# A RetNet and mixture-of-experts kernel: token tile 1 begun before expert 3 of tile 0, with batch 1's attention in token pairs

## The chip, the core and the metric

The kernel runs on one core of a Trainium2 chip. The core has a matrix engine (TensorE, PE in the profile), a vector engine (VectorE, DVE), a scalar engine (ScalarE, ACT), a general engine (GpSimd, POOL), a sync engine that issues transfers (SyncE, SP), and 16 DMA engines shared by all transfer queues. The metric is the device time of one execution in microseconds. It was 516.28 us, the median of six runs that lie between 514.69 and 517.29.

## What is computed

Two layers follow each other. The first is a retention attention over 8 batches, 8 heads, 576 positions and 64 dimensions: scores are multiplied by a decay instead of going through a softmax. The second is a mixture of four experts over the 4608 rows that come out, in which every expert works on every row.

```python
scores = scale * np.matmul(q, k.transpose(0, 1, 3, 2))
Dmat = np.where(rel >= 0, gamma[:, None, None] ** rel[None, :, :], 0.0)
attn = np.matmul(scores * Dmat[None], v)                 # [8, 8, 576, 64]
x = attn.transpose(0, 2, 1, 3).reshape(4608, 512)
p = domain_probs / (domain_probs.sum(-1, keepdims=True) + 1e-09)
for e in range(4):
    h = np.maximum(x @ w1[e], 0.0)                        # 512 -> 1024
    out += p[:, e:e + 1] * (h @ w2[e])                    # 1024 -> 512
```

## The kernel before

**Tiles and stages.** The 4608 rows are nine tiles of 512. A stage (nt, e) is one tile with one expert: the up product (512 to 1024 with ReLU, into the hidden tile `hT`) and the down product of the stage before, woven into it. A stage exists in two forms. The classical one (`up_classical`, `downs`) uses 32 products of 512 columns for up and 32 for down. The fast one (`up_fast`, `Down`) works by a seven-product scheme on halves of the matrices: 56 products of 256 columns each, with sums of the weights (`weight_sums`, `down_sums`), of the tokens (`token_sums`) and of the hidden tile (`hidden_sum`) that DVE makes. In `up_fast` each stage has two groups, and a quarter of the hidden tile gets its ReLU on POOL (the MIN/MAX in L716).

**Attention.** Chunks of 128 positions: scores (`S`), a mask, values (`O`), and a running state of keys times values (`sbd`), by which a later chunk sees the earlier ones. Four chunks make 512 positions and the remaining 64 (`Trem`, `Srem`, `Orem`) are handled apart. Class `Att` does whole chunks. Class `AttP` does token pairs: a unit is 256 positions (a half `hf`) by four heads (`u`), loaded with two neighbouring positions in a row of 512 bytes. Before the change only batch 0 is in pairs.

**What sets the order.** The order is written out by hand, engine by engine; each engine works through its own list, and a wait holds all that stands behind it on that engine. The head is the attention of batch 0, with warm-up products on PE between its parts (`warm`). Then classical stages run as a list of generators (`head`), counted in groups: one block of 128 hidden columns of an up product, or one block of 128 rows of a down product. `plan` and `at(g, ...)` hang other work behind group g, such as the casts, transposes and visits of batch 1 and the weight sums. From stage (1, 1) on a loop runs the fast stages. Between the quarters of a stage it calls `fill`, `sums`, `between` and `window`, which take attention work of batches 2 to 7 from lists (`Chain`) and the sums still owed from `owed`.

```python
begin = {1: (1, 1), 2: (1, 2), 3: (1, 3), 0: (2, 0)}
for nt, e in [(nt, e) for nt in range(1, n_nt) for e in range(E)][1:]:
    fast = before >= begin[before[1]]
```

**Transfers.** Weights are loaded on POOL's queue (fp32 in memory, bf16 on chip). Everything for tile 0's first stages and then all other experts is issued in one go at about 20 us. The inputs q, k, v go through SP's queue into buffers. Batch 0's remainder is gated on the landing of w2[0] and batch 1 follows it in order. Outputs are kept on chip over the four experts for tile 0 and the last tile (`on_chip`). For the others each stage sends its part, first plainly through SP, then by an accumulating transfer on POOL's queue (`send`).

## Time and profile before

| what | value |
|---|---|
| median of six runs | 516.28 us |
| the profiled execution, its own time | 515.51 us |
| its span, first to last instruction | 513.7 us |
| granted TensorE clock | 0.999 |
| instructions on PE, DVE, ACT, POOL | 4934, 696, 693, 345 |
| moved by DMA | 76.27 MB, 148 GB/s over the span |

The span is what the profile shows; the time of the execution is 1.8 us more. Profile times count from the span's start. In the lines of the profile, "L691" is line 691 of the kernel and "out<-in" names the tiles written and read. The page's busy times are sums over the whole span. The stretches (busy time of each engine between two times) show in their columns: the stretch, its length, PE, the weight loads of PE, DVE, ACT and POOL with the number of instructions, the granted clock, the share of the DMA engines and GB/s.

### The profile page before, as it was taken

The page shows a single profiled execution, that of the slowest core. Times are in us where ns is not written, and L with a number is a line of the kernel's source. Part 1 is how long each engine was busy: PE and PEld are TensorE (multiplying, and loading weights), DVE is VectorE, ACT ScalarE, POOL GpSimd, SP SyncE. Part 2 cuts the span into 40 slices and gives each one's busy share as a digit, 9 for nine tenths or more (in the row PEclk, how much of TensorE's full clock was granted, in tenths as well). Part 3 has the DMA queues.
Part 4 walks back from the last instruction along what each step waited for, and adds up shares of the span by engine and source line. Part 5 has one row for each costly group of instructions (what it writes and reads, how often), then busy time and mean ns, then how long its engine had stood idle before and what let it go on. Part 6 is the DMA issues. An engine that isn't in the chain of part 4 may idle for free.

```text
span 513.7 us, 12806 instructions
## 1 busy us (share of the span) xinstructions
PE 502.7 (98%) x4934; PEld 405.1 (79%) x4934; DVE 374.6 (73%) x696; ACT 336.1 (65%) x693; POOL 250.6 (49%) x345
## 2 busy tenths in 40 slices
PE   7999999999999999999999999999999999999995
PEld 3644455688888888888888888888888888888885
DVE  6625579778777777768777877886778777667775
ACT  3452254677667766777767776777777767767663
POOL 6702285656644756466645664476457521321012
PEclk9999999999999999999999999999999999999999
DMA  9999997949697699869998989789986652555002
GB/s 238 194 207 200 205 211 178 165 141 193 111 175 194 117 170 162 187 141 184 132 224 139 170 136 224 156 146 153 171 197 122 94 84 84 83 85 82 1 2 82
DMA packets 160749, 76.27 MB, mean 148 GB/s; under 512 B 131724, under 2 KB 144524, under 8 KB 160688
## 3 DMA queue, kind: packets, MB, share of 16 engines
q1 hardware_dynamic: 141648, 44.79, 43.7%
q0 software_dynamic: 18752, 30.41, 37.9%
q8 instruction: 38, 0.62, 0.5%
q10 hardware_dynamic: 288, 0.26, 0.2%
q14 instruction: 23, 0.19, 0.1%
HBM read 45.16 MB, written 31.46 MB: 149 GB/s over the span
## 4 chain that ended last, share of the span: by engine, by line
PE 91%; DVE 5%; DMA 1%; issue 1%; SPq 0%; ACT 0%; DVEq 0%; ACTq 0%
PE upP L691 21%; PE downV L645 20%; PE downW L645 15%; PE upR L691 10%; PE ph L525 7%; PE po L564 6%; PE upQ L691 5%; PE s L328 2%; PE oc L379 1%; PE kvp L346 1%; PE oc L376 1%; DMA raw<-in_q_dram 1%; DVE sT L469 1%; DVE sT L333 0%; DVE upR L707 0%
## 5 line engine op out<-in xcount | busy, mean ns | idle before, releaser
L691 PEld LDWEIGHTS <-wt 128*128 128x128 bf16 x992 | 94.9, 98 | 14.9 <-issue 1.9
L645 PEld LDWEIGHTS <-hT 128*128 128x128 bf16 x960 | 93.7, 98 | 12.0
L716 POOL TENSOR_SCALAR hT<-hT 128x512 bf16<-128x512 bf16 x62 | 38.2, 615 | 109.2 <-DVE hT L715 109.0
L645 PE MATMUL downV<-wt,hT 128*128 128x256 bf16 x480 | 81.8, 272 | 0.0
L691 PEld LDWEIGHTS <-wsum 128*128 128x128 bf16 x744 | 72.6, 98 | 9.1 <-issue 0.2
L707 DVE TENSOR_TENSOR upR<-upP,m 128x512 f32<-128x512 f32 x62 | 43.3, 698 | 49.0 <-ACT downW L651 39.9
L645 PEld LDWEIGHTS <-hsum 128*128 128x128 bf16 x720 | 70.0, 98 | 8.8 <-DVE hsum L617 0.3
L691 PE MATMUL upP<-xT,wt 128*128 128x256 bf16 x496 | 74.4, 272 | 1.1 <-DVE upR L707 0.6
L723 ACT ACTIVATE hT<-upP 128x512 bf16<-128x512 f32 x62 | 37.0, 597 | 52.0 <-PE upP L691 36.8
L514 POOL DMA_DIRECT2D out_dram<-acc x42 | 51.3, 1221 | 30.6 <-ACT acc L672 23.8
L674 DVE TENSOR_SCALAR acc<-downV,probs 128x512 f32<-128x512 f32 x56 | 41.9, 748 | 30.1 <-PE downV L645 29.7
L718 ACT ACTIVATE hT<-upR 128x512 bf16<-128x512 f32 x62 | 37.0, 597 | 31.7 <-PE upR L691 31.7
L709 ACT ACTIVATE hT<-upQ 128x512 bf16<-128x512 f32 x62 | 37.0, 597 | 15.9 <-PE upQ L691 15.9
L715 DVE TENSOR_TENSOR hT<-upP,m 128x512 bf16<-128x512 f32 x62 | 42.7, 689 | 6.0 <-PE upP L691 4.7
L672 ACT ACTIVATE acc<-downW,probs 128x512 f32<-128x512 f32 x56 | 38.6, 690 | 9.1 <-PE downW L645 9.1
L340 POOL TENSOR_SCALAR_AFFINE_SELECT sT<-sT 128x512 bf16<-128x512 bf16 x24 | 15.5, 646 | 58.0 <-ACT sT L339 48.6
L541 ACT ACTIVATE hT<-ph 128x512 bf16<-128x512 f32 x40 | 23.5, 597 | 29.8 <-PE ph L525 29.8
L697 ACT ACTIVATE upQ<-upP 128x512 f32<-128x512 f32 x62 | 37.0, 597 | 2.5 <-PE upP L691 2.3
L691 PE MATMUL upP<-tsum,wt 128*128 128x256 bf16 x248 | 37.3, 273 | 0.0
L691 PE MATMUL upR<-tsum,wsum 128*128 128x256 bf16 x248 | 37.2, 273 | 0.1
L691 PE MATMUL upP<-tsum,wsum 128*128 128x256 bf16 x248 | 37.2, 273 | 0.0
L691 PE MATMUL upQ<-xT,wt 128*128 128x256 bf16 x248 | 37.2, 273 | 0.0
(149 smaller groups left out, 1030.7 us busy)
## 6 DMA issues: line engine op xcount, KB each, us to landing
out_dram<-acc POOLq DMA_DIRECT2D x42, 512.0 KB, 6.4
out_dram<-acc SPq DMA_DIRECT2D x14, 512.0 KB, 4.1
wt<-in_moe_w_dram POOLq DMA_DIRECT2D x6, 1024.0 KB, 25.2
raw_k<-in_k_dram SPq DMA_DIRECT2D x24, 256.0 KB, 4.6
raw_q<-in_q_dram SPq DMA_DIRECT2D x24, 256.0 KB, 3.5
raw_v<-in_v_dram SPq DMA_DIRECT2D x24, 256.0 KB, 4.2
raw<-in_k_dram SPq DMA_DIRECT2D x8, 256.0 KB, 5.0
raw<-in_q_dram SPq DMA_DIRECT2D x8, 256.0 KB, 5.6
```

What stands on the lines that cost most here:

```text
L514: i = nc.gpsimd.dma_start(out=out_rows[:, x, :], in_=acc[nt, j], accum_op=ADD)
L645: nc.tensor.matmul(o, lhsT=l[:, k, self.s * 128:(self.s + 1) * 128], rhs=r[:, k], start=(i == 1 and k == 0), stop=(k == NFC // 2 - 1), ski ...
L672: nc.scalar.activation(a, po, Copy, scale=pe)
L674: nc.vector.tensor_scalar_mul(a, po, pe)
L691: nc.tensor.matmul(ps[:, l], lhsT=wa(kc)[:, f:f + 128], rhs=xa(kc), start=(start and l == 0 and kc == 0), stop=(kc == 1), skip_group_check ...
L697: nc.scalar.activation(Q, P, Copy)
L707: nc.vector.tensor_tensor(R_, P, m5, op=ADD)
L709: nc.scalar.activation(hT[:, lo, t0], Q, Relu)
L715: nc.vector.tensor_tensor(h22, P, m5, op=ADD)
L716: nc.gpsimd.tensor_scalar(h22, h22, float("inf"), 0.0, op0=MIN, op1=MAX)
L718: nc.scalar.activation(hT[:, lo, t1], R_, Relu)
L723: nc.scalar.activation(hT[:, hi, t0], P, Relu)
```

## The change

- Tile 0 runs experts 0, 1 and 2 classically. Then come stages (1, 0), (1, 1) and (0, 3), all fast, then (1, 2), (1, 3) and so on. Only the down product of (0, 2) is still classical beside a fast stage, with its quarters spread 8, 2, 2, 4 in the first group.
- Batch 1 is worked in token pairs by a new class `AttQ`. Its units are visited in the order 0, 2, 1, 3 (both halves of the first four heads, then of the others), between groups 25 and 31, and the last values product stands inside stage (1, 0).
- Batch 0's remainder moves from groups 29, 31, 34 to 22, 23, 24.
- The loads of batch 1 are gated on the first half of w1[2]. w2[2] is issued by POOL between two casts of batch 1, and w1[3] and w2[3] after its last cast. The raw buffers are taken from places that are free at that time.
- Batch 1's remainder is cast on POOL at the first gap of stage (1, 0). Batch 2's visits start after 16 gaps, which is in stage (0, 3).
- Weight and token sums get new places: those for experts 0 and 1 and tile 0 behind groups 9 to 31, those for experts 2 and 3 in stages (1, 0), (1, 1) and (0, 3).
- Outputs of tile 0 stay on chip for experts 0 and 1 only and are then sent; experts 2 and 3 are added by accumulating transfers.
- Eight more warm-up products stand in the head.

```diff
+    raw_x = xpool.tile([128, 2, H * D], FP32, tag="xT", name="raw")
     def raw_units(b):
         state[b] = {}
         for x in range(4):
-            t = wpool.tile([128, 3, H * D], FP32, tag=f"w2s_{x}", name="raw")
+            if b and x == 0:
+                t = [raw_x[:, 0], raw_x[:, 1], raw.tile([128, H * D], FP32, tag="raw", name="raw")]
+            elif b and x == 1:
+                t = [hpool.tile([128, H * D], FP32, tag=f"hs{i}", name="raw", bufs=1) for i in (1, 2, 4)]
+            else:
+                t = wpool.tile([128, 3, H * D], FP32, tag=f"w2s_{x}", name="raw")
+                t = [t[:, i] for i in range(3)]
...
+    class AttQ(AttP):
+        rem_states = (0, 1, 2, 3)
+        def visit(self, new, old):
+            ko = [one_bank(t, [128, 2, C + D], FP32, "ko") for t in ("a2", "o0")]
+            quads = [(a, j, d, c) for a in range(2) for j in range(2) for d in range(2) for c in range(2)]
+            if new:
+                hf, u = new
+                for a, j, d, c in quads:
+                    r, h = slice(64 * c, 64 * c + 64), 2 * a + d
+                    nc.tensor.matmul(ko[c][64 * d:64 * d + 64, a, C:], lhsT=self.m["k", hf, u][r, j, h, :],
+                                     rhs=self.m["v", hf][r, j, 4 * u + h, :], start=(a == 0 and j == 0),
+                                     stop=(j == 1), skip_group_check=True)
+                s = [one_bank(t, [128, 2, 2, C], FP32, "s") for t in ("a0", "a1")]
...
+            if old:
+                self.values(*old, ko)
...
-    def on_chip(nt):
-        return nt in (0, n_nt - 1)
+    def adds(nt, e):
+        return e > 0 and (nt == n_nt - 1 or (nt, e) == (0, 1))
+    def sends(nt, e):
+        return nt < n_nt - 1 and (nt, e) != (0, 0)
...
-    warm(8)
+    warm(10)
...
         a0.kv(hf, u)
+        if x < 3:
+            warm(2)
...
-    for e in range(2, E):
-        load_w1(e)
-        load_w2(e)
+    w12 = load_w1(2, 1)
+    load_w1(2, 0)
     load_next(w20)
...
-    for c in range(2):
-        for n in "kqv":
-            load_piece(1, n, c)
+    ORDER1 = (0, 2, 1, 3)
+    for x in ORDER1:
+        load_unit(1, x, w12)
...
-                    ok = n <= nt + 2
+                    ok = n <= (nt if (0, 3) in hTs else 0) + 2
...
+    at(3, lambda: cast1(0, "kv"), lambda: load_w2(2), lambda: cast1(1, "kv"), lambda: cast1(2, "kv"))
+    at(22, lambda: cast1(0, "q"), a0.Trem)
+    at(23, a0.Srem, a0.Srem_mask)
+    at(24, a0.Orem, lambda: a0.x(NCH, nc.scalar), lambda: a1.T(*UNITS[0]))
+    for i in range(4):
+        if i < 3:
+            at(24 + 2 * i, lambda i=i: cast1(i + 1, "q"))
+        at(25 + 2 * i, lambda i=i: visit1(i, i - 1))
+        if i < 3:
+            at(25 + 2 * i, lambda i=i: a1.T(*UNITS[ORDER1[i + 1]]))
+    at(25, lambda: cast1(3, "kv"), lambda: load_w1(3, 0), lambda: load_w1(3, 1), lambda: load_w2(3))
+    at(29, lambda: load_ahead(6))
...
+    stages = [(1, 0), (1, 1), (0, 3)] + [(nt, e) for nt in range(1, n_nt) for e in range(E)][2:]
+    owed = [((1, 0), (1, 1), t0[2])]
+    owed += [((1, 0), (1, 2), f) for f in ws[2][1:]]
+    owed += [((1, 0), (0, 3), f) for f in weight_sums(3)]
+    owed += [((1, 1), (1, 2), f) for f in down_sums(3)]
+    owed += [((1, 1), (1, 3), f) for f in down_sums(2)]
...
+            if gaps == 1:
+                rem1_casts()
+            if gaps == 13:
+                rem1_keys()
+            if i == 3 and gaps > 4:
+                pool(nt, 4 if gaps < 16 else 3 - g)
             if i == 3 or chain.todo["PE"] and "any" in chain.todo["PE"][0][1]:
-                chain.emit("PE", nt)
+                if gaps > 16:
+                    chain.emit("PE", nt)
...
+                for n in range((8, 2, 2, 4)[i - 1] if g == 0 else 4):
+                    if (g, i, n) == (0, 1, 4):
+                        visit1(4, 3)
+                        t1.pop(0)()
+                        front.extend(t1)
```

## The prediction

> **What bounds the kernel now.** I read the page's busy times and clock first, then busy time by stretch of the span, the chain of work, the DMA queues by stretch, and last the waits of GpSimd (POOL).

> ```profile
> PE 502.7 (98%) x4934; PEld 405.1 (79%) x4934; DVE 374.6 (73%) x696; ACT 336.1 (65%) x693; POOL 250.6 (49%) x345
> PEclk9999999999999999999999999999999999999999
> ```

> TensorE (PE) is busy all the time at the full clock. Where it has gaps is shown by the stretches (PE's busy time is the second number):

> ```profile
> 0.00:20.00 20.00, 15.58 (x229) 9.23 (x230) 13.80 (x35) 7.56 (x19) 14.95 (x31) 1.00 1.01 221
> 20.00:47.45 27.45, 27.45 (x142) 13.50 (x140) 9.45 (x16) 12.08 (x20) 5.47 (x7) 1.00 1.21 202
> 47.45:62.00 14.55, 14.55 (x89) 6.81 (x87) 7.36 (x14) 4.78 (x8) 1.83 (x3) 1.00 1.19 209
> 62.00:89.40 27.40, 27.16 (x245) 14.57 (x244) 23.40 (x36) 13.84 (x27) 18.91 (x21) 1.00 0.92 196
> 89.40:140.00 50.60, 49.77 (x481) 39.55 (x480) 41.04 (x71) 34.68 (x69) 30.94 (x40) 1.00 0.85 152
> 140.00:500.00 360.00, 359.62 (x3683) 314.19 (x3682) 271.35 (x509) 258.28 (x539) 175.07 (x241) 1.00 0.78 136
> ```

> From 20 us on PE loses 0.24 us before stage (1, 1) begins at 89.4, 0.83 us up to 140 and 0.38 us from there to 500. So the kernel gets faster by less PE work or not at all, and any new wait of PE adds to the time in full. The chain gives the prices of a piece:

> ```profile
> 33.64 13.81 PE po L564 x64
> 47.45 5.18 PE ph L525 x24
> 52.63 0.34 PE ptr L319 x8
> 65.63 0.45 PE ptc L309 x8
> 66.94 0.33 PE s L328 x8
> 67.27 0.24 PE kvp L346 x8
> 205.25 0.44 PE upP L691 x4
> ```

> A 512-column product takes 0.216 us (13.81/64), a 256-column one 0.109 (0.44/4). The third thing to see is how the two DMA queues share the engines; q0 carries the weights (issued by POOL), q1 what SP issues. The queues' packets, MB and share, first from 24 to 30 us, then from 42 to 46 us:

> ```profile
> q0 software_dynamic: 1233, 1.23, 124.0%
> ```

> ```profile
> q0 software_dynamic: 608, 0.62, 91.4%
> q1 hardware_dynamic: 606, 0.15, 29.4%
> ```

> Alone, the weights move 205 packets of 1 KB per us, 1 MB in 5 us. Shared, the queues go packet for packet, 152 per us each, so SP's small packets crawl. The last view is POOL's waits:

> ```profile
> POOL hT L716 <- DVE hT L715: 109.0, 41, 5.7
> ...
> POOL krb L287 <- DMA raw_k<-in_k_dram: 18.2, 1, 18.2
> ```

> POOL stood 18.2 us at one cast whose load crawled under the weights. It was harmless there, because the queue behind it was not urgent. The change puts POOL in that place again.

> **The change, part by part.**

> 1. *Fewer classical products.* Two up stages, (0, 3) and (1, 0), and the two down stages that belong to them become seven-product ones. Out go 120 products of 512 columns (25.9 us), 8 of 384 (0.163 each by their row, 1.3) and 8 of 128 (0.056, 0.45): 27.65. In come 224 of 256 columns: 224 x 0.109 = 24.45. That is -3.2 us, all on PE's path. [...]

> 2. *Batch 1 in token pairs.* Its 32 transposes stay 32. Scores were 32 products in four pieces of 0.33 (1.3 us); now they are 64, and batch 0's same form took 0.35 for 16 (1.4). Key-value products: 32 in four pieces of 0.24 (1.0) become 64 of 64 columns, between 0.24 and 0.35 per 16 (1.0 to 1.4). Values: 32 at 0.37 per 8 against 64 at 0.35 per 16, the same. State products go from 12 to 24 at 0.056 (+0.7). Batch 1's remainder reads four states instead of one: 12 x 0.029 = +0.35. Sum +1.2, between +1.0 and +1.7.

> 3. *Warm-up products:* eight more at 0.216, 1.7 us of PE in the head. Two stand before the first transposes, where PE waited 1.1 us for the query cast; the other pairs stand where it waited 0.57, 0.20 and 0.20. The two small waits are overrun by 0.23 each, but the transposes there feed a DVE that is still masking scores. Without that cover they cost 0.46. I take +0.1, between 0 and 0.5. They could also gain: the six runs lie at 514.7 to 514.9 and at 516.3 to 517.3, and one reading is a head that some executions run at a lower clock. The profiled execution shows no such drop, so I count nothing and keep -1.5 for the range.

> 4. *Old idle time:* the 0.24 us before 89.4 and the 0.4 us of the mask pile-up at 93.4 go, since batch 1 is finished before. The bulk payments of weight sums on DVE at about 112 us are replaced by similar ones. I take -0.6, between 0 and -1.

> 5. *Loads of batch 1.* All twelve are now wanted by PE at about 50 to 60 us instead of 65 to 77. They wait for the first half of w1[2]; the whole landed at 42.2 (issued 20.10, 22.1 us to landing), so that half lands at about 39.6. q0 runs dry at about 42. Batch 0's remainder (1536 packets of 256 bytes) is through by about 42.5. From there a 256 KB load takes 0.9 us: in the head q1 moved such packets at 297 GB/s. POOL casts the remainder and the first unit and issues w2[2] at about 47.3; its packets begin 2 us later, when seven loads are through. The other five share with w2[2]: 1024 packets at 152 per us are 6.7 us, in which two loads pass, then three more at 0.9. Landings: third unit's values 56.9, last unit's keys, queries, values 57.8, 58.7, 59.6. PE, without waits, starts up(0, 2) at 47.45 + 0.34 + 0.12 for the remainder moved ahead of it, and needs the third unit's cast values at 57.1 (6 x 0.86 of up, 0.55 remainder, 3 x 0.45 transposes, two visits 2.3). With POOL's cast of 0.61 it gets them at 57.5; the last unit's transposes then wait for DVE's query cast (58.7 + 0.75) about 0.3. I take +0.7, between 0 and +4 (the loads moved behind all of w2[2]).

> 6. *Remainder of batch 1 on POOL.* Its casts stand in front of the MIN/MAX of the first hidden tile of stage (1, 0). Behind that stand the hidden sums on DVE, behind them the DVE addition that frees PE's bank. On q1 two output sends stand ahead of its loads; 512 KB took 1.35 us there (0.38 MB/us at 105 to 108 us), so they are through at 61.3. w1[3] is issued after the last values cast, its packets begin at about 62.3. So one microsecond is left alone at 820 packets per us; the rest (about 700) shares, 4.6 us. The last piece lands at about 68. It is needed by 72: stage (1, 0) begins at 62.6, its last bank is wanted 12.6 later, less 0.4 cast, 0.6 MIN/MAX, 2 x 0.42 hidden sums, a 0.69 weight sum and the 0.69 addition. I take +0.1. If all 1536 packets share, or crawl as batch 0's did (10.2 to 16.3 us from issue), it is up to +5.

> 7. *First visit inside stage (1, 0):* last values to ScalarE copies (three, 0.25 to 0.38) to a 0.42 token sum to PE, against 0.86 + 0.44 of cover: +0.1. Weight sums of expert 3 want w1[3] at about 71; it lands at about 70. Four more POOL output sends (1.2 each) lie in POOL's idle half. The stages after (1, 1) keep their pattern of visits.

> Sum: -3.2 + 1.2 + 0.1 - 0.6 + 0.7 + 0.1 + 0.1 = -1.6 us. The profiled execution took 515.51, so it would take 513.9; the median of the runs shown is 0.77 above it, and against 516.28 I predict 514.6.

> **Rivals.** (a) *POOL stuck at batch 1's remainder*, slower: it decides as soon as the last piece lands after 72 us. Issued at about 61 and crawling like batch 0's values it lands at 77.3; cast, MIN/MAX, sums and addition end at 80.5 instead of 75.2. That is 5.3 us on -1.6: 520.0. For it: the 18.2 us row, and 2 MB of weights on q0 at that very time. Against: one microsecond of free queue is enough. (b) *Unit loads later*: w2[2] overtakes three more loads, and the last unit is 2 us later. This gives 516.7. For it: POOL may issue w2[2] earlier than I have it. Against: its issue waits for a cast that comes late in the same chain. (c) *Everything hidden*: parts 5 to 7 at zero and all old idle time gone, -3.0: 513.3. For it: my margins in parts 5 and 6 are under 1 us.

> **How the numbers follow.** A measurement of this kernel tells about 0.3% (1.55 us) from no change. Forecast 0.40, own range 513.4 to 515.6 (0.31 of it under 514.73, faster; 0.09 within). (c) 0.12, faster. (b) 0.18 (0.13 within, 0.05 slower). (a) 0.30, slower. So faster 0.43, within 0.22, slower 0.35. The range goes from (c) less half of the 1.5 us of part 3, 512.6, to (a), 520.0.

> **What would show it.** 224 more matmuls of 256 columns at 0.109 and 120 fewer of 512: part 1. PE's waits for DVE's query casts and for GpSimd's values casts near 57 to 60 us, together under 1 us: part 5. GpSimd's wait at krb and vbd ending before 72 us, and no DVE hidden sum that waits for GpSimd in stage (1, 0): part 6; a wait of several microseconds there is rival (a). Stage (1, 1) should begin at about 76.5 us; each microsecond later is a microsecond lost. The prediction is wrong if PE's gaps between 47 and 90 us add up to over 2 us.

## The result, and the profile after

The changed kernel is slower. Its median is 518.21 us (22 runs between 515.87 and 521.01) against 515.73 us of the kernel before (46 runs between 514.59 and 519.27); the ratio is 1.0052, with a 95% interval of 1.0040 to 1.0064. The prediction had been 514.6. The profiled execution took 519.62 us (its span is 517.9), where the prediction's sum had 513.9; it is 1.4 us above the median.

From the page of the changed kernel: busy times, the clock over the span, and the shares of the chain.

```profile
PE 505.0 (98%) x5150; PEld 416.6 (80%) x5150; DVE 383.9 (74%) x722; ACT 348.5 (67%) x736; POOL 252.9 (49%) x351
PEclk9999899999999999999999999999999999999999
PE 88%; DVE 4%; DMA 3%; issue 2%; ACT 1%; SPq 1%; POOL 0%; DVEq 0%; ACTq 0%; POOLq 0%
```

A digit 8 now stands in the fifth slice of the clock (about 52 to 65 us), and transfers have 3% of the chain. The stretches of the changed kernel, with PE's busy time second and the granted clock before the DMA share:

```profile
20.50:47.45 26.95, 26.95 (x141) 13.01 (x139) 17.63 (x30) 12.10 (x20) 5.35 (x8) 1.00 1.22 219
47.45:62.00 14.55, 10.85 (x207) 6.30 (x204) 6.88 (x14) 9.54 (x30) 5.87 (x7) 0.94 1.12 250
62.00:75.00 13.00, 12.36 (x131) 7.47 (x132) 7.03 (x15) 7.18 (x18) 5.85 (x9) 0.80 1.12 183
75.00:90.00 15.00, 14.77 (x116) 11.08 (x114) 14.01 (x22) 9.87 (x20) 10.31 (x10) 1.00 0.96 183
```

From 20.5 to 47 us PE loses nothing. Then it loses 3.7 us in one stretch and works with a clock of 0.94 and 0.80 in two. PE's waits from 20 to 100 us (total, times, longest):

```profile
PE pt L517 <- DVE qm L433: 3.8, 1, 3.8
PE upP L772 <- DVE hT L796: 0.7, 1, 0.7
PE upP L772 <- DVE upR L788: 0.5, 2, 0.3
```

The long one is that of the last unit's transposes (`pt`) for the query cast. The delay is 4.0 us, not 3.8: a product's recorded end lies 0.16 us behind the moment at which the next can start (eight `ph` products of 0.216 are recorded as 1.89 us and not as 1.73). From here on the text gives waits with these 0.16 us, and the lines show them without. The chain of work around it (start, length, what):

```profile
48.72 12.66 DMA raw<-in_q_dram
...
61.47 0.70 DVE qm L433
62.18 0.05 issue
62.22 1.03 PE pt L517 x8
63.25 3.41 PE ph L609 x8
```

The last unit's queries take 12.66 us from issue to landing, where those of the third unit take 5.4. The clock record shows half speed from 60.25 us, still in the wait, for 6.83 us: behind the wait eight `ph` products take 3.41 us where they otherwise take 1.73 (0.216 each), eight transposes 1.03 where they otherwise take 0.45. The queues from 50 to 57 us (packets, MB, share):

```profile
q0 software_dynamic: 825, 0.84, 83.4%
q1 hardware_dynamic: 780, 0.39, 26.1%
```

In those 7 us w2[2] on q0 and batch 1's loads on q1 go nearly packet for packet, but at 118 and 111 a us, not at the 152 of the prediction. Without w2[2] beside them, q1 moved 574 of these 512-byte packets from 49 to 50 us.

Stage (1, 1) starts at 82.57 us, where the prediction had 76.5. From there to the span's end it is 435.3 us (517.9 - 82.57), where the prediction had 435.6 (513.9 less the 1.8 outside the span, less 76.5). So the whole loss of this execution lies ahead of 82.6 us.

### The profile page after: what moved, and what is told of

The parts are those of the page before. It is cut to its first block, busy times and chain, and to the rows that moved or that the text cites. A ratio compares the mean times of both kernels' runs of the same rounds, so it can differ in the third digit from the quotient of the medians.

```text
span 517.9 us, 13354 instructions
## 1 busy us (share of the span) xinstructions
PE 505.0 (98%) x5150; PEld 416.6 (80%) x5150; DVE 383.9 (74%) x722; ACT 348.5 (67%) x736; POOL 252.9 (49%) x351
## 4 chain that ended last, share of the span: by engine, by line
PE 88%; DVE 4%; DMA 3%; issue 2%; ACT 1%; SPq 1%; POOL 0%; DVEq 0%; ACTq 0%; POOLq 0%
PE upP L772 22%; PE downV L726 21%; PE downW L726 16%; PE upR L772 11%; PE upQ L772 5%; DMA raw<-in_q_dram 3%; PE ph L609 3%; PE po L645 3%; PE s L340 2%; PE oc L391 1%; PE kvp L358 1%; PE oc L388 1%; DVE sT L482 1%; DVE upR L788 1%; SPq L113 1%
## 5 line engine op out<-in xcount | busy, mean ns | idle before, releaser
L772 PEld LDWEIGHTS <-wt 128*128 128x128 bf16 x1056 | 101.0, 98 | 16.7 <-issue 2.9
L726 PEld LDWEIGHTS <-hT 128*128 128x128 bf16 x1024 | 100.0, 98 | 12.8
L797 POOL TENSOR_SCALAR hT<-hT 128x512 bf16<-128x512 bf16 x66 | 41.3, 625 | 115.7 <-DVE hT L796 115.4
L726 PE MATMUL downV<-wt,hT 128*128 128x256 bf16 x512 | 87.2, 272 | 0.0
L772 PEld LDWEIGHTS <-wsum 128*128 128x128 bf16 x792 | 77.3, 98 | 9.6
L788 DVE TENSOR_TENSOR upR<-upP,m 128x512 f32<-128x512 f32 x66 | 46.1, 698 | 50.1 <-ACT downW L732 41.3
L726 PEld LDWEIGHTS <-hsum 128*128 128x128 bf16 x768 | 74.7, 98 | 9.1
L772 PE MATMUL upP<-xT,wt 128*128 128x256 bf16 x528 | 79.2, 272 | 1.0 <-DVE xT L676 0.5
L804 ACT ACTIVATE hT<-upP 128x512 bf16<-128x512 f32 x66 | 39.4, 597 | 53.7 <-PE upP L772 38.8
L598 POOL DMA_DIRECT2D out_dram<-acc x46 | 56.2, 1221 | 33.8 <-ACT acc L753 27.0
L755 DVE TENSOR_SCALAR acc<-downV,probs 128x512 f32<-128x512 f32 x60 | 44.9, 748 | 31.5 <-PE downV L726 31.0
L352 POOL TENSOR_SCALAR_AFFINE_SELECT sT<-sT 128x512 bf16<-128x512 bf16 x24 | 15.5, 646 | 59.2 <-ACT sT L351 50.3
L772 PE MATMUL upP<-tsum,wt 128*128 128x256 bf16 x264 | 39.6, 273 | 0.7 <-DVE hT L796 0.7
L772 PE MATMUL upP<-tsum,wsum 128*128 128x256 bf16 x264 | 39.6, 273 | 0.0
L772 PE MATMUL upR<-tsum,wsum 128*128 128x256 bf16 x264 | 39.6, 273 | 0.0
L772 PE MATMUL upR<-xT,wsum 128*128 128x256 bf16 x264 | 39.6, 273 | 0.0
L772 PE MATMUL upQ<-xT,wt 128*128 128x256 bf16 x264 | 39.6, 273 | 0.0
```

The source lines that it names most:

```text
L598: i = nc.gpsimd.dma_start(out=out_rows[:, x, :], in_=acc[nt, j], accum_op=ADD)
L726: nc.tensor.matmul(o, lhsT=l[:, k, self.s * 128:(self.s + 1) * 128], rhs=r[:, k], start=(i == 1 and k == 0), stop=(k == NFC // 2 - 1), ski ...
L755: nc.vector.tensor_scalar_mul(a, po, pe)
L772: nc.tensor.matmul(ps[:, l], lhsT=wa(kc)[:, f:f + 128], rhs=xa(kc), start=(start and l == 0 and kc == 0), stop=(kc == 1), skip_group_check ...
L788: nc.vector.tensor_tensor(R_, P, m5, op=ADD)
L797: nc.gpsimd.tensor_scalar(h22, h22, float("inf"), 0.0, op0=MIN, op1=MAX)
```

## The experiments

Times are medians of runs beside the kernel before on the same chip, with the ratio to it and its 95% interval. The theory: two sets of loads, batch 1's units (3 MB) and w2[2] (1 MB), are wanted by about 62 us, the transfers cannot bring both, and what comes last is waited for; the wait also halves PE's clock (for 6.83 us in the changed kernel). The first rival: the place of w2[2] in POOL's queue alone is at fault. Others are that the new PE work costs more than it was priced, and that the wait, not the clock, carries all of the loss.

**w2[2] later, and w2[2] first.**

```diff
# e1_w2_late
-    at(3, lambda: cast1(0, "kv"), lambda: load_w2(2), lambda: cast1(1, "kv"), lambda: cast1(2, "kv"))
+    at(3, lambda: cast1(0, "kv"), lambda: cast1(1, "kv"), lambda: cast1(2, "kv"), lambda: load_w2(2))
# e4_w2_first: taken out of at(3, ...), and
     load_w1(2, 0)
+    load_w2(2)
     load_next(w20)
```

> The load of w2[2] is issued behind the casts of batch 1's third unit instead of in front of those of the second; nothing is left out. Theory (w2[2] pushes the last unit's loads behind it, TensorE waits for the last query cast and then runs at half clock): the last queries land at about 55 us instead of 61.4, the wait of TensorE at the fourth transposes falls from 3.8 us to under 1, the clock stays at full, w2[2] lands at about 62 and costs at most 1 us at the first classical down product of stage (1, 0). Median about 514 us, 4 us under the changed kernel. Rival (the loss is in the paired attention or on GpSimd and the wait only shows it): stage (1, 1) still begins at 82 us or later, median 517 to 519.

> The load of w2[2] is issued with the first burst, right behind w1[2]; nothing is left out. Theory (the transfers are the limit: bytes of batch 1 and of w2[2] together must pass before the last queries): the last queries still land at 58 to 61 us, and the units before come later too; median 517 to 520. Rival (the order on GpSimd is the cause: its issue between two casts): the wait falls under 1 us and the median to about 514.

PE's longest wait in e1 and in e4:

```profile
PE po L645 <- DMA wt<-in_moe_w_dram: 4.1, 1, 4.1
```

```profile
PE sr L400 <- DVE kbd L315: 5.1, 1, 5.1
```

e1: 518.09, 1.0058 (1.0040 to 1.0076). The last unit's queries land at 53.7 and its transposes do not wait, but w2[2] lands at 65.57 and the first down product waits for it. e4: 519.99, 1.0093 (1.0072 to 1.0115). w2[2] is early, and the first unit is late: its queries land at 51.2. Their cast stands in VectorE's list ahead of the copies of batch 0's remainder (`kbd`), and PE waits for these from 47.5 us. These two places only choose who waits, and for them the rival falls.

**Filling the wait.**

```diff
# e2_fill_wait (18) and e7_fill_8 (8), ahead of the last unit's transposes
+            if i == 2:
+                at(29, lambda: warm(18))
             at(25 + 2 * i, lambda i=i: a1.T(*UNITS[ORDER1[i + 1]]))
```

> 18 warm-up products (3.9 us at full clock) stand in front of the fourth unit's transposes, where TensorE waits 3.8 us in the changed kernel; nothing else moves. Theory (the half clock after the wait is a cost of its own): the clock stays at full from 47 to 75 us, the transposes still come at about 62.2, stage (1, 0) begins at about 65.2 instead of 67.6, median 516. Rival (the low clock costs nothing, or it comes from something else than the wait): median 518 or more, the clock low as before.

> Eight warm products (8 x 0.216 = 1.7 us of TensorE work on constants) stand in front of the last unit's transposes, in the place of the first part of the 4.0 us wait. [...] Rival (the half clock is shown in the records but costs nothing, or the filler's own time adds): 518 or more, as with eighteen products.

e2: 518.23, 1.0061 (1.0046 to 1.0076). The clock stays at 1.0, and from the transposes to stage (1, 0) it is 3.1 us (63.10 to 66.19) against 5.4 in the changed kernel (62.22 to 67.61): the half clock costs 2.3 us there. Nothing is won, since in this execution the queries had landed at 58.4 and the filler itself was the delay. The clock is not all of the loss: seven of the 22 runs of the changed kernel have a mean granted clock of 0.998 or more (one stretch of 3.41 us at half speed takes 0.003), and they lie between 515.87 and 520.75 us, still above the 515.73 of the kernel before. e7: 517.67, 1.0056 (1.0026 to 1.0085). Stage (1, 1) starts at 79.50, 3.1 us earlier than in the changed kernel, and yet the time is nearly the same: a wait of 2.3 us at 91 us, with the clock at half for 3.4 us behind it, takes it back. This was the first sign of a second limit.

**The warm-up products.**

```diff
# e3_old_warm
-    warm(10)
+    warm(8)
-        if x < 3:
-            warm(2)
```

> The eight added warm-up products of the head are taken out again, all else as changed. Theory (they are hidden in waits of the head): the first up products begin within 0.2 us of the changed kernel's, median 518 give or take 0.7. Rival 1 (they delay the head): 0.5 to 1.7 us faster. Rival 2 (without them the head falls to a lower clock in some executions): 1 us or more slower.

518.49, 1.0067 (1.0043 to 1.0090), like the changed kernel: the eight products are not the loss.

**The load of w2[2] left out.** e5 fills the tile with a constant on VectorE at the start, e9 on GpSimd while it is idle.

```diff
# e9_no_w2_pool
     load_w1(2, 0)
+    w2_none = wpool.tile([128, NFC, Dm], BF16, tag="w2_2", name="wt2")
+    nc.gpsimd.memset(w2_none, 0.01)
     load_next(w20)
-    at(3, lambda: cast1(0, "kv"), lambda: load_w2(2), lambda: cast1(1, "kv"), lambda: cast1(2, "kv"))
+    at(3, lambda: cast1(0, "kv"), lambda: w2_sb.append(w2_none), lambda: cast1(1, "kv"), lambda: cast1(2, "kv"))
```

> Leaves out the load of expert 2's w2 (1 MB): its tile is filled with a constant by VectorE in the first microseconds, so expert 2's down products are computed with wrong weights but in the same number. Theory (two sets of loads, batch 1's units and w2[2], are both wanted by about 62 us, and the DMA engines cannot bring both): with 1 MB less in the queue the last unit lands by 55, neither the transposes of the last unit nor the first down products of expert 2 wait over 1 us, the clock stays 1.0, stage (1,0) starts at about 61 and stage (1,1) at 75.8 to 76.5. The profiled execution is 435.3 us from there to the span's end plus 1.7 outside it: 512.8 to 513.5, 1.5 to 2.5 us under the kernel before. Rival 1 (the token pairs of stage (1,0) or the visits themselves cost more than was priced): (1,1) starts at 78 or later and the time is over 515. Rival 2 (w2[2] has no part in the late landing; 512-byte pieces are slow by themselves): the queries of the last unit still land after 58, 517 or more.

> As e5_no_w2 (the load of expert 2's w2 left out, its tile filled with a constant, so the products of expert 2 are done with wrong weights), but the fill stands on GpSimd between 25 and 35 us, where it has nothing to do, and not ahead of VectorE's first work, where it put everything 3.9 us back. Theory: with 1 MB less, no wait over 1 us up to stage (1,1), which starts at 75.8 to 76.5; what then bounds is the chain of batch 2's loads, the value cast on GpSimd and the second output of (0,2) behind it near 92 us, which may take 0.5 to 2 us: 512.8 to 515. Rival (stages cost more than they were priced, whatever the loads do): (1,1) at 78 or later.

e5 misses: 516.69, 1.0014 (0.9995 to 1.0032). Its fill took 3.47 us ahead of VectorE's first work, and the first transposes began at 9.78 in place of 5.71. e9: 513.09, 0.9953 (0.9935 to 0.9970), faster than before. PE's waits from 40 to 100 us and two stretches of e9:

```profile
PE upP L772 <- DVE hT L796: 0.7, 1, 0.7
PE upP L772 <- DVE upR L788: 0.5, 2, 0.3
```

```profile
47.45:62.00 14.55, 14.46 (x278) 8.87 (x278) 10.24 (x20) 11.86 (x38) 11.54 (x13) 1.00 1.19 271
62.00:75.00 13.00, 12.57 (x104) 8.35 (x102) 9.72 (x19) 8.61 (x18) 2.41 (x3) 1.00 1.20 204
```

The wait and the half clock are gone and stage (1, 1) starts at 75.99. The 6.63 us between the two profiled executions (519.62 and 512.99) are 0.3 us in the head, 4.0 of wait and 2.3 of half clock. So the PE work is, in sum, what it was priced at, and 1 MB of transfers makes the difference.

**Keeping the outputs away from w2[2].**

```diff
# e6_w2_out1: as e1, and in send(); e8_w2_outs: without the j
             i = nc.sync.dma_start(out=out_rows[:, x, :], in_=acc[nt, j])
+            if (nt, e, j) == (0, 1, 1):
+                after(i, w2_dma[2])
```

> As e1_w2_late (w2[2] issued after the last unit's keys and values of the third visit are cast, 52.5 us), and the second output of (0,1), with batch 1's remainder behind it on SP's queue, starts only once w2[2] has landed. Theory: w2[2] then shares only with the last loads of the units and the first output, 1.5 MB from 53.5 at about 180 KB/us, and lands at 61 to 62 in place of 65.6, so the wait of 4.07 us at the first down product goes, the clock stays 1.0, (1,1) starts at 76 to 77, and the profiled execution is 513.3 to 514.5. Rival (the transfers are the limit wherever they stand): the second output lands at 66 or later and the accumulator that it frees, or the remainder of batch 1 after 72, takes over 2 us of the gain: 515.5 to 517.5.

> As e6_w2_out1, but both outputs of (0,1) start only once w2[2] has landed. Theory: w2[2] lands at 59 to 60, no wait at the down products; the first output lands at about 64.5 and its accumulator is wanted at about 62.5, so up to 2 us of wait comes there, without a drop of the clock: 514 to 516. Rival: the outputs and the remainder behind them come so late (the remainder over 72) that the time stays at 517 or more.

Both much worse: 524.21, 1.0159 (1.0142 to 1.0177), and 526.57, 1.0203 (1.0185 to 1.0222). The chain of e6:

```profile
64.64 13.09 DMA raw_q<-in_q_dram
77.73 0.07 issue
77.80 0.33 POOL qrb L301
```

w2[2] lands at 63.4 and is waited for by 0.7 us only. But the remainder of batch 1, behind the held output on SP's queue, now crawls beside the 2 MB of expert 3 and lands at 77.7. PE waits 6.3 us for what hangs behind it. In e8 the first output lands at 70.1, and PE already waits 5.4 us from 67 us on. The wait in e6 is the prediction's rival (a), produced by the gate.

**Fewer bytes: expert 2 of tile 0 added on chip.**

```diff
# e10_keep; e11_keep_late: the same with e1's line
-        return e > 0 and (nt == n_nt - 1 or (nt, e) == (0, 1))
+        return e > 0 and (nt == n_nt - 1 or (nt, e) in ((0, 1), (0, 2)))
-        return nt < n_nt - 1 and (nt, e) != (0, 0)
+        return nt < n_nt - 1 and (nt, e) not in ((0, 0), (0, 1))
-            i = nc.sync.dma_start(out=out_rows[:, x, :], in_=acc[nt, j])
+            i = (nc.gpsimd if (nt, e) == (0, 2) else nc.sync).dma_start(out=out_rows[:, x, :], in_=acc[nt, j])
```

> Expert 2 of tile 0 is added on chip to the accumulators of experts 0 and 1 (VectorE evacuates its products in place of ScalarE), so the two outputs of (0,1), 1 MB of writes between 50 and 65 us, go, and the outputs of (0,2) are plain writes. w2[2] stays where the changed kernel has it. Theory: the last unit's loads stand ahead of those outputs in one queue and gain little from it: the queries land at 60 to 61.4, the wait stays over 2.5 us, and the time is 516.5 to 518. Rival (the outputs share the engines with the last loads): the queries land by 59, the wait is under 1.5 us and the clock stays 1.0, 514 to 515.5.

> e10_keep and e1_w2_late together: no outputs of (0,1), and w2[2] issued at 52.5 us behind the casts of the third unit. In e1 its packets began to move only when the outputs' writes were through (55.9), and then shared with the remainder of batch 1 at 152 packets each a us. Theory: they begin at 54.6 and share with the remainder alone, 1024 packets at 152/us, so w2[2] lands at 61.5 to 62.7 and the first down product, wanted at 61.5, waits under 1.2 us; the clock stays 1.0, (1,1) starts at 76 to 77, and the time is 513 to 515. Rival (a wait moves further back: the remainder after 66, w1[3] after 71, or the accumulators near 92): over 516.

e10: 518.85, 1.0071 (1.0036 to 1.0106), above the range of either side. The queries land at 59.9 and the gap is 1.8 us, between the two expectations, and with VectorE's four evacuations come gaps of 1.2 and 1.1 us at 78 and 84 us. e11: 516.75, 1.0029 (1.0017 to 1.0041). The wait for w2[2], landed at 63.84, is 2.5 us with the clock at half for 3.4 us behind it, and the VectorE gaps are there too.

**w2[2] in two halves.** The first four down products need one half only.

```diff
# load_w2(e, part) loads blocks part * NFC // 2 to (part + 1) * NFC // 2; at(3, ...) becomes
# e12_split
+    at(3, lambda: cast1(0, "kv"), lambda: cast1(1, "kv"), lambda: load_w2(2, 0), lambda: load_w2(2, 1), lambda: cast1(2, "kv"))
# e13_split_two
+    at(3, lambda: cast1(0, "kv"), lambda: cast1(1, "kv"), lambda: load_w2(2, 0), lambda: cast1(2, "kv"), lambda: load_w2(2, 1))
# e14_split_late
+    at(3, lambda: cast1(0, "kv"), lambda: cast1(1, "kv"), lambda: cast1(2, "kv"), lambda: load_w2(2, 0), lambda: load_w2(2, 1))
```

> w2[2] is loaded in two halves (four of its eight blocks each), both issued behind the casts of the second unit, at about 50.3 and 51.2 us: 2.6 us later than in the changed kernel, 2.3 us sooner than in e1. All bytes are moved. Theory (place and first need decide; there are 3 us of slack between the last unit's landing in e1, 54.6, and its transposes, 57.9): the last unit lands at 57 to 58.5 and its transposes wait 0.5 to 1.5 us; the first half lands by 60 (wanted 61.2) and the second by 63 (wanted 63.3); the clock stays 1.0; (1,1) starts at 76.5 to 77.5 and the time is 513.5 to 515. Rival (the sum of bytes is the limit): the waits still add up to over 3 us before stage (1,1), 516.5 or more.

> w2[2] in two halves, the first issued behind the second unit's casts (50.3), the second behind the third's (about 53.5). Theory: the transposes of the last unit wait under 0.7 us, the first half lands by 60.5, the second at 63 to 64.5 and is waited for by 0 to 1.2 us in the middle of the first block of down products; clock 1.0, (1,1) at 76.5 to 77.5, 513.5 to 515. Rival: waits of over 3 us in all, 516.5 or more.

> As e1_w2_late, with w2[2] in two halves. Theory: the first half lands at 61 to 62 (wanted 61.5), the second at about 65.5 to 66 (wanted 63.3), so the one wait of 4.07 us becomes two of 0.5 and 2.2 us, none long enough to halve the clock; (1,1) at 78.5 to 79.5, 515 to 516.5. Rival (the split changes nothing): 517.5 or more, with the clock at half for 3.4 us.

e12: 518.85, 1.0060 (1.0044 to 1.0076). e13: 517.04, 1.0033 (1.0020 to 1.0046). e14: 517.31, 1.0033 (1.0017 to 1.0049). All three miss their range. In e14 the one wait does become two, of 0.5 and 1.5 us, and stage (1, 1) starts at 77.7; a wait of 2.3 us at 87 us follows. In e12 and e13 the theory holds up to stage (1, 1), which starts at 76.74 and 76.52 with no wait over 0.6 us before it, and all bytes are moved. The loss is behind it. Two of PE's waits in e13, and GpSimd's and VectorE's work ahead of the first, which ends at 90.72 us (in brackets the idle time before an instruction, and what ended it):

```profile
PE upP L773 <- DVE hT L797: 3.1, 1, 3.1
PE downV L727 <- DVE acc L756: 1.4, 1, 1.4
```

```profile
83.36 0.97 POOL L294 CAST vm<-raw_v 128x512 bf16<-128x512 f32 x1 [2.02 <-PE upP L773]
84.51 1.28 POOL L292 TENSOR_TENSOR km<-raw_k,gk 128x512 bf16<-128x512 f32 x1 [0.17 <-DMA raw_k<-in_k_dram]
85.73 1.23 POOL L599 DMA_DIRECT2D out_dram<-acc  x1
86.58 1.06 POOL L798 TENSOR_SCALAR hT<-hT 128x512 bf16<-128x512 bf16 x1
```

```profile
87.67 1.26 DVE L699 TENSOR_TENSOR hsum<-hT 128x512 bf16<-128x512 bf16 x1 [1.82 <-POOL hT L798]
...
89.98 0.68 DVE L797 TENSOR_TENSOR hT<-upP,m 128x512 bf16<-128x512 f32 x1
```

Four casts of batch 2 (two are shown) wait for loads that are themselves late: they are issued from 71.75 us on, when the remainder of batch 1, landed at 64.9 to 71.4, is through. Behind the casts stand, in GpSimd's queue, the issue of the second output of (0, 2) and then the MIN/MAX of a quarter of the hidden tile. The hidden sum on VectorE waits for the MIN/MAX, and behind that sum stands the addition (L797) that frees PE's bank. It is the path of the prediction's rival (a), with batch 2's casts in the place of the remainder's. e12 and e7 show the same path at 88 and 91 us. The output itself lands at 93.54 and frees its accumulator only for the second wait, at 93 us. The expectation of e15, below, takes the first wait for the accumulator's. The changed kernel has a wait of 0.87 us at 93.9 in front of the same products, but there VectorE does not wait for GpSimd.

**The output ahead of the casts.**

```diff
# e16_out_only on the changed kernel, e15_out_first on e13
-            if i == 3 and gaps > 4:
+            if i == (4 if gaps < 9 else 3) and gaps > 4:
                 pool(nt, 4 if gaps < 16 else 3 - g)
```

> e13_split_two, and in GpSimd's queue the second output of (0,2) stands ahead of the four casts of batch 2 that it stood behind (keys, queries and values of one piece and the keys of the next). In e13 its accumulator was ready at about 77, it was issued at 84.5 because the casts waited for batch 2's loads, and the accumulator came free at 90.7, 3.2 us late. Theory: it is issued at 77 to 78.5, its accumulator is free by 86, the wait at 87 falls under 1 us and the one of 1.5 us at 92.8 with it, stage (0,3) starts at about 90, and the time is 512.5 to 514.5, faster than both kernels. Rival (the casts, 1.2 us later, hold up batch 2's attention, or the transfers are simply too many up to 95 us): the same wait in another place, 516 or more.

> The changed kernel with that one move in GpSimd's queue (the output ahead of four casts of batch 2) and w2[2] where it was. Theory: the first wait (4.0 us) and the half clock stay, the wait of 0.87 us at 93.9 goes: (1,1) at 82 to 83, 516.8 to 517.8. Rival (the second place matters only when stage (1,1) starts early): no change, 518.2.

e15: 516.52, 1.0030 (1.0014 to 1.0046). The output is issued at 78.4, the MIN/MAX ends at 86.3 and not at 87.6, and the wait at 88 us shrinks from 3.2 us to 1.2. PE comes to it 1.5 us later than in e13 and leaves it 0.5 us sooner. Five gaps between 0.5 and 1.2 us are left between 51 and 93 us, and the time is not below the kernel before. e16: 518.08, 1.0049 (1.0022 to 1.0075), beside the 518.2 of its rival and the 517.8 at most of its theory: with these runs the two cannot be told apart. For they go from 514.95 to 524.18, and the profiled one is the 514.95: no wait for the queries over 0.2 us, clock at 1.0. In it POOL issues w2[2] 0.26 us behind the last unit's keys (48.30 and 48.04), and the queries land at 58.5. In the changed kernel's profiled execution w2[2] comes 0.24 us ahead of those keys (47.67 and 47.91), and the queries land at 61.4. The other profiled executions with w2[2] in that place land between these or close to them: 0.10 ahead, 60.9 (e3); 0.10, 0.11 and 0.15 behind, 60.6 (e7), 58.4 (e2) and 59.9 (e10). So half a microsecond between two queues goes with up to 3 us of landing: in the changed kernel the loads ahead of w2[2] moved about five times as fast as those beside it (574 packets a us against 111). That this also makes the changed kernel's spread of 5 us is an inference; only the profiled executions show landings.

**All of it together.** Both kernels have e10's outputs and e16's order.

```diff
# e17_all_late: e10 + e14 + e16; e18_all_two: e10 + e13 + e16
```

> The outputs of (0,1) kept on chip (as e10), w2[2] in two halves behind the third unit's casts (as e14), and the second output of (0,2) ahead of batch 2's casts in GpSimd's queue (as e15). Theory: without the outputs the first half of w2[2] lands at 59.5 to 61 and the second at 63 to 64 (wanted 61.5 and 63.3), the remainder by 61, so stage (1,1) starts at 76.5 to 78 with the 1.2 us of waits that VectorE's evacuations brought in e10 and e11, nothing over 1.2 us is waited for near 88, and the time is 513.5 to 515.2. Rival (VectorE's work in stage (1,0) is the next limit): waits of over 3 us between 65 and 100 us, 516 or more.

> As e17_all_late, with the halves of w2[2] around the third unit's casts (as e13 and e15). Theory: both halves land before they are wanted, at the price of a later last unit and remainder (a wait of up to 1 us at the transposes, as in e15): 513.5 to 515.5. Rival: as for e17_all_late, 516 or more.

e17: 519.15, 1.0078 (1.0057 to 1.0099). e18: 519.66, 1.0074 (1.0055 to 1.0093). Both rivals: stage (1, 1) starts at 77.4 and 77.3, with every load in time, and then PE waits 3.4 us at 81 us. VectorE's and GpSimd's work of e17 at that time:

```profile
78.26 0.41 DVE L699 TENSOR_TENSOR hsum<-hT 128x512 bf16<-128x512 bf16 x1
78.71 0.42 DVE L701 TENSOR_TENSOR hsum<-hsum,hT 128x512 bf16<-128x512 bf16 x1
79.22 4.38 DVE L705 TENSOR_TENSOR hsum<-hT,hsum 128x1024 bf16<-128x1024 bf16 x1
83.53 0.69 DVE L789 TENSOR_TENSOR upR<-upP,m 128x512 f32<-128x512 f32 x1
```

```profile
79.45 1.06 POOL L292 TENSOR_TENSOR km<-raw_k,gk 128x512 bf16<-128x512 f32 x1
80.45 1.05 POOL L292 TENSOR_TENSOR qm<-raw_q,gq 128x512 bf16<-128x512 f32 x1
81.44 0.61 POOL L294 CAST vm<-raw_v 128x512 bf16<-128x512 f32 x1
82.01 1.04 POOL L292 TENSOR_TENSOR km<-raw_k,gk 128x512 bf16<-128x512 f32 x1
```

The hidden sum that takes 0.69 us elsewhere (e13 at 95.3 us) takes 4.38 here, and ends half a us after four casts that GpSimd does without a gap. The loads are in time now, so the casts no longer wait for them and run in one block beside VectorE. No kernel with all of its loads came out below the kernel before. Left open, and not tried, are w2[2] at about 49 us, between the places of e16 (48.3) and e13 (50.0), with the output ahead of the casts, and the MIN/MAX ahead of batch 2's casts.

## Why the prediction was wrong

Wrong sign: 1.7 us faster was forecast, 2.5 us slower is what the medians give (518.21 - 515.73). (The sum of -1.6 against 516.28 is 514.7, not 514.6; nothing hangs on it.) The prediction's own sign of being wrong, more than 2 us of gaps of PE between 47 and 90 us, came true with 4.0 in one wait.

- *Parts 1 to 4 and 7* (PE's work, token pairs, warm-ups, old idle time, the visit inside stage (1, 0)): right in sum. Without parts 5 and 6 they give 515.51 - 2.4 = 513.1, and e9 took 512.99. The counts are as forecast: `po` products go from 160 to 96 and `ph` products of 512 columns from 140 to 84, which is the 120, and 224 of 256 columns come in. Part 3's warm-ups are neutral within its bounds (e3). Gaps of 0.4, 0.4 and 0.9 us at 72.8, 85.9 and 93.9 us were not foreseen and stand in e9's time too, so some other term was about as much too dear; which one was not separated.
- *Part 5* is the step that failed. "I take +0.7, between 0 and +4": its own wait of 0.3 us at the last unit's transposes was 4.0. The issue of w2[2] was right (47.67 against 47.3). Nearly nine loads, not seven, were through ahead of its packets (4435 packets of 512 bytes by 50.1 us), which helped. But the sharing ran at 118 and 111 packets a us instead of 152 each, a price taken from 256-byte packets and used for 512-byte ones, and the end dragged on: the last of the 512-byte packets still moved after 61 us. So the queries landed at 61.4 instead of 58.7 (2.7 us), and PE was ready 0.95 us sooner than the prediction had it: 0.3 + 2.7 + 0.95 is the wait.
- *The missing term* is the clock. With the wait of 4.0 us came 6.83 us at half clock, 2 of them still in the wait, and the rest cost 2.3 us. The prediction looked at the clock only in the head, and an upper bound of +4 for part 5 was therefore too low: such a wait costs 6.3. That is this execution; between the medians of the changed kernel and of e9 it is 5.1 (518.21 and 513.09).
- *Part 6 and rival (a)*: the last piece of the remainder landed at 66.6 (forecast 68, wanted by 72), and GpSimd stood there for 0.6 us only. In e6 it landed at 78, and rival (a) came with 6.3 us of wait. The margin was real, and its deadline too.
- *Rival (b)* had the right place, a later last unit, with a price of 2 us; the wait and the clock made it 6. *Rival (c)*, 513.3, is what e9 shows when 1 MB is left out.
- *What the prediction had not asked*: whether the changed order can be fed at all. e1, e4, e6, e12 and e13 each take the wait at 58 us away and show another, at 62, 47, 76, 88 and 88 us. From 20 to 62 us the DMA engines are busy throughout (shares of 1.12 to 1.22 in the stretches above), and in the median of every version with all of its loads the 2.4 us of work saved came back as waits. The share alone does not tell: e9 has 1.19 and 1.20 and hardly waits.

## What to carry to other kernels

Before work is pulled forward, sum the bytes that are wanted by then against what the queues move together: here the DMA engines were busy from 20 to 62 us (shares of 1.12 to 1.22), and the 2.4 us saved on TensorE came back as waits. Price a long wait of PE with the clock too: in these executions the 11 windows of 3.41 us at full clock in which PE was busy for 0.46 of the time or less, between 20 and 500 us, were each followed by half clock, which cost 2.3 us in the changed kernel. Price a load that shares with another queue by its own packet size: the 512-byte packets moved at 111 a us where the 152 of 256-byte ones had been taken. When one late load is cured, look for the next thing that was hidden behind it (in e13 a MIN/MAX of 1.06 us behind casts in the same queue, in e17 a hidden sum of 4.38 us beside four casts) before counting the gain.

## What the hardware showed that was not expected

```profile
90.80:94.21 3.41, 1.27 (x13) 0.99 (x11) 3.31 (x7) 0.72 (x2) 2.04 (x5) 1.00 1.19 211
```

```profile
79.22:82.63 3.41, 1.79 (x17) 1.46 (x15) 3.41 (x1) 1.53 (x4) 3.38 (x5) 1.00 0.68 210
82.63:86.04 3.41, 1.84 (x17) 1.66 (x17) 3.31 (x6) 0.60 (x1) 0.70 (x2) 1.00 0.65 133
```

  PE is busy for 0.37 of the first and for 0.52 and 0.54 of the others. A window at half clock in which PE was busy for 0.42 (the changed kernel) or 0.63 (e12) was followed by another, one with 0.92 (e17) by full clock.
- *512-byte packets moved slower beside w2[2] than the price taken from 256-byte ones.* Beside the 1 KB packets of w2[2], the packets of batch 1's loads, 512 bytes each, moved at 33 to 138 a us (51 to 57 us in the changed kernel) against 574 without it (49 to 50 us). In the kernel before, 256-byte packets moved at 152 a us beside the weights (42 to 46 us).
- *VectorE beside GpSimd.* A hidden sum on VectorE (128x1024) took 4.38 us instead of 0.69 while GpSimd ran four casts in a row (e17; 4.37 in e18). The 20 profiled executions hold 658 such hidden sums: the 13 that lie beside a cast on GpSimd take 0.70 to 4.38 us, and none of the others takes longer than 0.70. In e17 the sum is recorded as started at 79.22, 0.23 us ahead of the first cast (GpSimd was still issuing an output, beside which alone such a sum takes 0.69 us), and it ends at 83.60, 0.55 us behind the end of the fourth. What makes it so long was not shown.
